# A Fourier, channel-mix and Mish kernel on one core: the ScalarE order of its first stage, the start of its weight conversion, and the first pair of its channel mix

## The chip, the cores and the metric

The kernel runs on one core of a Trainium2 chip. The metric is device time in microseconds (us) for one execution; lower is better. Engines are named as in the profile: PE is TensorE's matmul stream and PEld its weight loads, DVE is VectorE, ACT is ScalarE, POOL is GpSimd, SP is SyncE, whose queue issues nearly all DMAs here. Each engine works through its own queue in order and waits on semaphores of the others.

## The reference

```python
def _attn_ref(x, w_r, w_i, b_r, b_i):                  # x: 4 x 3072 x 256
    X = np.fft.rfft(x, axis=1)
    Yr = Xr @ w_r - Xi @ w_i + b_r
    Yi = Xr @ w_i + Xi @ w_r + b_i
    Yr = np.sign(Yr) * np.maximum(np.abs(Yr) - 0.01, 0.0)
    Yi = np.sign(Yi) * np.maximum(np.abs(Yi) - 0.01, 0.0)
    return np.fft.irfft(Yr + 1j * Yi, n=3072, axis=1)

def _moe_ref(x, mu_k, mu_r, w_k, w_v, w_r):            # channel mix, d_ff 1024
    x_prev = x shifted by one step, zero first
    xk = mu_k * x + (1.0 - mu_k) * x_prev
    xr = mu_r * x + (1.0 - mu_r) * x_prev
    k = np.maximum(xk @ w_k, 0.0)
    return 1.0 / (1.0 + np.exp(-(xr @ w_r))) * (k * k @ w_v)

def _moe2_ref(x, w_in, w_out):                         # Mish, d_ff 2048
    h = x @ w_in
    return (h * np.tanh(log1p(exp(h)))) @ w_out
```

The three run one after the other on 12288 tokens of 256 channels. The weights of the last two are float64 and are turned into float32 on the core.

## The kernel before

Three stages follow each other. **The first stage** does the Fourier part and takes roughly the first 295 us. **The second** (the loop over `t` at line 865) does the channel mix, and **the third** (line 1128) the Mish part. Large products are made from a high part (`h`, rounded to float32r) and a low part (`l`, the rest): three matmuls, high by high, high by low and low by high, stand for one.

The first stage is the loop over `u` at line 667, called a turn here: 48 turns (`NU`), each one group of 256 rows of one batch, and 3 more to finish. The order of a turn is written by hand, and every engine gets its instructions in that order. A turn holds these steps:

- `s2(u + 2)` (line 345): 8 PE matmuls, second half of the DFT, into the single PSUM tile `s2p`. `s2_ev` (365): ACT copies it to `Xf` (line 368), then POOL adds real and imaginary part as a third part of `Xf` (371).
- `high_X(u + 2)` (373): ACT casts `Xf` to its high part `Xh` (375; two buffers). `low_X(u + 1)` (378): DVE subtracts to get `Xl` (381).
- `mix(u)` (392): 18 PE matmuls of `Xh` and `Xl` with the weights `WX`, the first six into `k1p` (one PSUM tile) and the rest into `mxp`. DVE adds the bias to `k1p` (411, result `yt`), and `mix_ev` adds `mxp` (425).
- `above(u)` (427): ACT rectifies `yt` less the threshold into `yc` (429). `shrink(u - 1)` (432): DVE makes `Y` of `yt` and `yc` (435). `swap` (437): three POOL copies exchange halves of `Y` (440 to 442).
- `is1(u - 2)` (444): 2 PE matmuls of the inverse DFT into `i1p`. `is1_ev(u - 3)` (455): ACT copies it to `Cs` (460), and SP stores it.
- In 20 of the turns (`S1_AT`), `s1` (298): 8 PE matmuls of the first half of the DFT of a later group (303). `s1_ev` in the next turn copies them on ACT (311), and SP stores them. Every seventh turn of each batch's twelve (`u % 12 == 6`) has 6 more matmuls in its mix.
- `bg(n)` (85): n steps of a queue of small jobs, 2 and 3 per turn with an `s1`, 1 and 1 in the others. The first jobs load three small tensors. Then `bg_weights` (108) converts nine blocks of the second stage's weights: it loads the first block (`dec_raw`, 512 KB), lets 4 steps pass, and then makes for each block seven DVE instructions (lines 140 to 159), one ACT cast (97) and one DVE subtraction (99).
- From turn 33 on `early(k)` (630) prepares the second stage: inverse DFT of the first tile (`is2`, PE line 509, copied by ACT at 518), its difference `dl` (529), and the two mixed inputs. `shift` (532) makes one of them on DVE (537) and returns a function that makes high part (ACT, line 77) and low part (DVE, line 78) in one step.

After the last mix come three `i1` steps with two `is2` steps between them; this is the drain. Then the second stage begins. It works in pairs `P` of 128-wide columns: `emit_k` (803) makes 12 matmuls per column pair into `kp`, `k_ev` (821) rectifies on ACT (825), squares twice on ACT (835, 836) and subtracts on DVE (837); `emit_v` two pairs later uses the result.

The order of the last steps of a turn, as far as the change touches it:

```python
        if u + 2 < NU:
            s2(u + 2)
        if u > 2:
            is1_ev(u - 3)
        ...
        if u + 2 < NU:
            s2_ev(u + 2)
        ...
        if u < NU:
            mix_ev()
            above(u)
        if u + 2 < NU:
            high_X(u + 2)
```

Of the kernel before, what the change touches and what calls it, by code (L numbers as in the profile page):

```python
# [8 lines left out]
F32 = mybir.dt.float32  # L9
# [3 lines left out]
AF = mybir.ActivationFunctionType  # L13
ALU = mybir.AluOpType
# [15 lines left out]
def kernel(  # L30
# [27 lines left out]
    nc = tc.nc  # L58
# [26 lines left out]
    def bg(n):  # L85

        while n > 0 and bgq:
            try:
                next(bgq[0])
                n -= 1  # L90
            except StopIteration:
                bgq.popleft()
# [15 lines left out]
    def bg_weights(pool, items):  # L108

        if items[0][0].dtype == F32:  # L110
            for src, hi, lo, f in items:
                yield from bg_weight(pool, src, hi, lo, f)
            return
        nxt = raw_load(pool, items[0][0], 2)
        for _ in range(4):
            yield
        for i, (src, hi, lo, f) in enumerate(items):
            raw = nxt
            if i + 1 < len(items):
                nxt = raw_load(pool, items[i + 1][0], 2)  # L120
            yield from bg_weight(pool, src, hi, lo, f, raw=raw)
# [60 lines left out]
    ps1p = ps1.__enter__()  # L182
# [298 lines left out]
    pE = [None]  # L481
# [50 lines left out]
    def shift(t, nm):  # L532
        dl = dl_t[0]
        mu = mk if nm == "xk" else mr
        f = pE[0].tile([128, 2, TA], F32, tag="xf", name="xf", bufs=2)
        for eh in range(2):
            nc.vector.scalar_tensor_tensor(
                out=f[:, eh, :].rearrange("p (m c) -> p m c", m=3), in0=dl[:, eh], scalar=mu[:, eh:eh + 1],
                in1=yv(0)[:, eh], op0=ALU.mult, op1=ALU.add,
            )  # L540
        hl = pE[0].tile([128, 2, 2, TA], F32R, tag=nm, name=nm, bufs=(2 if nm == "xk" else 1))
        (xk_t if nm == "xk" else xr_t)[t] = hl
        return lambda: split(f, hl[:, 0], hl[:, 1])

    warm(3)
    for q in range(8):
# [61 lines left out]
    WK = pkp.tile([128, 2, 2, FK], F32R, tag="WK", name="WK", bufs=1)  # L608
# [16 lines left out]
    def pe_half(t, eh, m0):  # L625
        p = ps1p.tile([128, 2, 256], F32, tag="s1", name="s1p")
        is2(t, eh, p, m0, 2)
        is2_ev(t, eh, m0, 2)

    def early(k):  # L630

        if k == 0:
            load_Dp(0)
            load_D(0)
            load_IF(0)
        elif k == 1:
            pass
        elif k == 2:
            load_D(1)
            load_IF(1)  # L640
        elif k == 3:
            new_yT()
            prefix(0, ps1p.tile([128, 2, 256], F32, tag="s1", name="s1p"))
            later[0] = prefix_ev()
        elif k < 8:
            if k == 4:
                later[0]()
            pe_half(0, (k - 4) // 2, 2 * ((k - 4) % 2))
        elif k == 8:
            delta()  # L650
            load_IF(2)
        elif k == 9:
            later[0] = shift(0, "xk")
        elif k == 10:
            later[0]()
            load_D(2)
        elif k == 11:
            later[0] = shift(0, "xr")
        elif k == 12:
            later[0]()  # L660
        elif k in (14, 15):
            for m0 in (0, 2):
                pe_half(1, k - 14, m0)

    later = {}
    U_E = 32
    for u in range(NU + 3):
        if u + 2 < NU:
            s2(u + 2)
        if u > 2:  # L670
            is1_ev(u - 3)
        if u + 1 < NU:
            low_X(u + 1)
        if 1 <= u <= NU:
            shrink(u - 1)
        while s1_t:
            s1_ev()
        if u + 2 < NU:
            s2_ev(u + 2)
        if 1 <= u <= NU:  # L680
            swap(u - 1)
        if u < NU:
            mix(u)
        if u > 2:
            bg(2 if u in S1_AT else 1)
        if u < NU:
            mix_ev()
            above(u)
        if u + 2 < NU:
            high_X(u + 2)  # L690
        if u + 5 < NU:
            load_A(u + 5)
        if NU <= u < NU + 2:
            early(u - U_E - 2)
        if u == 0:
            load_x(1, 6)
        if u in S1_AT:
            i = 8 + S1_AT[u]
            s1(*divmod(i, 8))
            if i + 3 < 8 * B:  # L700
                load_x(*divmod(i + 3, 8))
        if 2 <= u < NU + 2:
            is1(u - 2)
        if u > 2:
            bg(3 if u in S1_AT else 1)
        if u == U_E:
            p1s.__exit__(None, None, None)
            pEg = tc.tile_pool(name="pE", bufs=1, side="left", reuse_waits="tile")
            pE[0] = pEg.__enter__()
        if U_E < u < NU - 1:  # L710
            early(u - U_E - 1)
# [14 lines left out]
    pap = pa.__enter__()  # L726
    psa = tc.tile_pool(name="psa", bufs=1, space=PSUM, reuse_waits="tile")
    psap = psa.__enter__()
# [6 lines left out]
        src = w_out[q * 256:(q + 1) * 256, :].rearrange("(f p) n -> p f n", p=128)  # L735
        bgq.append(bg_weight(pap, src, WO[:, 2 * q:2 * q + 2, 0, :], WO[:, 2 * q:2 * q + 2, 1, :], 2))

    P3 = ((0, 0), (0, 1), (1, 0))
    g_t = {}

    def emit_h0(P):
# [7 lines left out]
    def h_mm(f0, p):  # L749
# [3 lines left out]
        for dh in range(2):  # L753
            for (w, v) in P3:
                nc.tensor.matmul(  # L755
# [26 lines left out]
    def emit_r(t):  # L782
        hl = xr_t.pop(t)
        p = psap.tile([128, 2, 512], F32, tag="p", name="pp")
        for o in range(2):
            i = 0
            for dh in range(2):
                for (w, v) in P3:
                    nc.tensor.matmul(  # L789
# [12 lines left out]

    def emit_k(P):
        t, i2 = divmod(P, 4)
        hl = xk_t[t]
        p = psap.tile([128, 2, 512], F32, tag="k", name="kp", bufs=2)
        for m in range(2):
            f = 2 * i2 + m
            i = 0
            for dh in range(2):  # L810
                for (w, v) in P3:
                    nc.tensor.matmul(  # L812
                        out=p[:, m, 0:TA], lhsT=WK[:, dh, w, f * 128:(f + 1) * 128], rhs=hl[:, v, dh, :],
                        start=(i == 0), stop=(i == 5),
                    )
                    i += 1
        kp_t[P] = p

    kp_t = {}

    def k_ev(P, then):
        p = kp_t.pop(P)
        v = p[:, :, 0:TA]
        kr = pap.tile([128, 2, TA], F32, tag="kf", name="kr", bufs=2)
        nc.scalar.activation(out=kr, in_=v, func=AF.Relu)
        if then:
            then()
        kh = pap.tile([128, 2, TA], F32R, tag="kh", name="kh", bufs=2)
        kl = pap.tile([128, 2, TA], F32R, tag="kl", name="kl", bufs=2)
        if False:  # L830

            nc.vector.scalar_tensor_tensor(out=kr, in0=v, scalar=0.0, in1=kr, op0=ALU.max, op1=ALU.mult)
            split(kr, kh, kl)
        else:
            nc.scalar.activation(out=kh, in_=kr, func=AF.Square)  # L835
            nc.scalar.activation(out=kr, in_=kr, func=AF.Square)  # L836
            nc.vector.tensor_tensor(out=kl, in0=kr, in1=kh, op=ALU.subtract)  # L837
        kk_t[P] = (kh, kl)

    def emit_v(P):  # L840
# [24 lines left out]
    for t in range(NA + 1):  # L865
# [5 lines left out]
        for i2 in range(4):  # L871
            P = 4 * t + i2
# [6 lines left out]
            then = None  # L879

            if nxt:
# [11 lines left out]
                elif i2 == 2:  # L893
# [5 lines left out]
                    then = shift(t + 1, "xk")  # L899
                else:  # L900
# [4 lines left out]
                    then = shift(t + 1, "xr")  # L905
# [10 lines left out]
            if t == NA - 1 and i2 == 0:  # L916
                hl = x2h_t[0] = w2p.tile([128, 2, 2, 512], F32R, tag="x2h", name="x2h", bufs=1)
# [210 lines left out]
    for P in range(2, 8 * NBLK + LAG):  # L1128
        t, q = divmod(P, 8)
# [111 lines left out]
```

## Time and profile before

| | us |
|---|---|
| median of 3 runs | 1973.39 (1970.25 to 1975.01) |
| the profiled execution's own time | 1974.12 |
| span of the profile, first to last instruction | 1972.3 |
| PE busy | 1946.8 (99%) |
| PEld busy | 1826.0 (93%) |
| DVE busy | 1360.9 (69%) |
| ACT busy | 1065.3 (54%) |
| POOL busy | 137.7 (7%) |

The profile is of one execution. Busy times are sums over the whole span; as matmuls are pipelined and their ends are modelled, a PE shown as busy may still be held up, so the distance from the start of one turn's mix to the start of the next is the better measure. Times in rows count from the span's start. The span is 1.8 us shorter than the execution's own time.

### The profile page before, as it was taken

To read this page: it belongs to the slowest core of one execution; us is meant where nothing else is said; L and a number is where in the kernel's file an instruction comes from. 1 tells how busy PE (TensorE), PEld (TensorE's weight loads), DVE (VectorE), ACT (ScalarE), POOL (GpSimd) and SP (SyncE) were. 2 spreads that over 40 slices of the span, in tenths; PEclk is the share of its full clock that TensorE was granted. 3 is DMA by queue.
4 is the path that set the end of the run, shared out by engine and by line. 5 is a ranking of instruction groups with operands and counts; after the bars stand their busy time and mean duration, and the time that the engine had idled before them with its cause. 6 is when DMAs were issued, how large, how long until landed. Compare 5 with 4: busy or idle time off the path is not lost.

```text
span 1972.3 us, 31894 instructions
## 1 busy us (share of the span) xinstructions
PE 1946.8 (99%) x12658; PEld 1826.0 (93%) x12658; DVE 1360.9 (69%) x2083; ACT 1065.3 (54%) x1598; POOL 137.7 (7%) x236
## 2 busy tenths in 40 slices
PE   7999989999999999999999999999999999999999
PEld 5788879999999999999899999999999999999998
DVE  3688765655656556554587877777877777887785
ACT  3466556666666666666544444444444444444444
POOL 1344440000000000000000000000000000000000
PEclk9999999999999999999999999999999999999999
DMA  9677532221221211210100100010000010000000
GB/s 292 176 235 233 158 100 69 68 62 58 60 62 58 71 60 50 71 58 17 48 23 22 29 26 22 23 33 22 29 27 22 23 33 22 29 27 22 22 12 22
DMA packets 71736, 122.94 MB, mean 62 GB/s; under 512 B 6370, under 2 KB 48580, under 8 KB 71588
## 3 DMA queue, kind: packets, MB, share of 16 engines
q1 hardware_dynamic: 68004, 108.33, 18.7%
q0 software_dynamic: 3584, 12.58, 1.8%
q8 instruction: 100, 1.64, 0.4%
q14 instruction: 48, 0.39, 0.1%
HBM read 70.56 MB, written 50.33 MB: 61 GB/s over the span
## 4 chain that ended last, share of the span: by engine, by line
PE 88%; issue 3%; DVE 3%; ACT 2%; POOL 2%; DMA 2%; SPq 0%; POOLq 0%; ACTq 0%; DVEq 0%
PE h L1057 20%; PE o L1105 18%; PE kp L812 14%; PE vp L850 13%; PE o L1106 9%; PE pp L789 3%; PE p L1057 3%; PE pp L509 3%; ACT Xh L375 1%; DMA XS<-in_x_dram 1%; PE hp L755 1%; PE mxp L408 1%; DVE Xl L381 1%; POOL sw L440 1%; POOL Xf L371 1%
## 5 line engine op out<-in xcount | busy, mean ns | idle before, releaser
L1105 PE MATMUL o<-WO,gh 128*128 128x512 f32 x1536 | 562.0, 394 | 0.0
L1106 PE MATMUL o<-WO,gl 128*128 128x256 f32 x1536 | 430.3, 280 | 0.0
L1057 PE MATMUL h<-xS,WS 128*128 128x256 f32 x2208 | 350.9, 281 | 0.0
L1105 PEld LDWEIGHTS o<-WO,gh 128*128 128x128 f32 x1536 | 288.9, 188 | 43.3
L1070 ACT COPY p1s<-p 128x256 f32<-128x256 f32 x184 | 68.8, 374 | 471.6 <-PE p L1057 470.6
L1057 PEld LDWEIGHTS h<-xS,WS 128*128 128x128 f32 x2208 | 299.6, 188 | 16.1
L812 PE MATMUL kp<-xk,WK 128*128 128x384 f32 x1536 | 294.1, 339 | 0.0
L837 DVE TENSOR_TENSOR kl<-kr,kh 128x768 fp32r<-128x768 f32 x128 | 123.0, 961 | 243.7 <-ACT kr L836 243.7
L1106 PEld LDWEIGHTS o<-WO,gl 128*128 128x128 f32 x1536 | 289.5, 188 | 0.2
L850 PE MATMUL vp<-kh,WV 128*128 128x384 f32 x1024 | 280.3, 335 | 0.0
L812 PEld LDWEIGHTS kp<-xk,WK 128*128 128x128 f32 x1536 | 266.2, 188 | 0.6 <-ACT yT L518 0.2
L1060 DVE TENSOR_TENSOR C<-h,p1s 128x512 f32<-128x512 f32 x184 | 127.2, 692 | 157.9 <-PE h L1057 157.9
L1042 DVE TENSOR_TENSOR gl<-g,gh 128x1024 fp32r<-128x1024 f32 x184 | 223.8, 1216 | 2.1 <-ACT g L1039 2.1
L1038 ACT ACTIVATE gh<-C 128x1024 fp32r<-128x1024 f32 x184 | 195.6, 1063 | 10.8 <-DVE C L1060 10.7
L1039 ACT ACTIVATE g<-C 128x1024 f32<-128x1024 f32 x184 | 193.0, 1049 | 0.0
L1057 PE MATMUL h<-xS,WI 128*128 128x256 f32 x1104 | 189.8, 280 | 0.0
L1060 DVE TENSOR_TENSOR C<-h,wu 128x512 f32<-128x512 f32 x368 | 187.7, 552 | 0.3 <-PE h L1057 0.3
L850 PEld LDWEIGHTS vp<-kh,WV 128*128 128x128 f32 x1024 | 186.7, 188 | 0.0
L850 PE MATMUL vp<-kl,WV 128*128 128x384 f32 x512 | 171.5, 335 | 0.0
L835 ACT ACTIVATE kh<-kr 128x768 fp32r<-128x768 f32 x128 | 108.2, 845 | 100.0 <-PE vp L850 99.9
L1057 PEld LDWEIGHTS h<-xS,WI 128*128 128x128 f32 x1104 | 155.7, 188 | 0.0
L1060 DVE TENSOR_TENSOR wu<-h,C 128x512 f32<-128x512 f32 x184 | 126.6, 688 | 35.3 <-PE h L1057 31.4
(145 smaller groups left out, 2607.9 us busy)
## 6 DMA issues: line engine op xcount, KB each, us to landing
scr<-Cs SPq DMA_DIRECT2D x48, 256.0 KB
D<-scr SPq DMA_DIRECT2D x32, 384.0 KB
x2d<-r POOLq DMA_DIRECT2D x32, 384.0 KB, 2.8
x<-x2d SPq DMA_DIRECT2D x24, 512.0 KB
out_dram<-ob SPq DMA_DIRECT2D x96, 128.0 KB
A<-scr SPq DMA_DIRECT2D x44, 256.0 KB
xs<-in_x_dram SPq DMA_DIRECT2D x24, 384.0 KB
scr<-xs SPq DMA_DIRECT2D x24, 384.0 KB
```

The costliest lines, as they stand in the source:

```text
L812: nc.tensor.matmul(out=p[:, m, 0:TA], lhsT=WK[:, dh, w, f * 128:(f + 1) * 128], rhs=hl[:, v, dh, :], start=(i == 0), stop=(i == 5),)
L835: nc.scalar.activation(out=kh, in_=kr, func=AF.Square)
L837: nc.vector.tensor_tensor(out=kl, in0=kr, in1=kh, op=ALU.subtract)
L850: nc.tensor.matmul(out=p[:, o, 0:TA], lhsT=WV[:, f, w, o * 128:(o + 1) * 128], rhs=v[:, m, :], start=(f == 0 and i == 0), stop=(f == 7 and ...
L1038: nc.scalar.activation(out=gh, in_=c, func=AF.Mish)
L1039: nc.scalar.activation(out=g, in_=c, func=AF.Mish)
L1042: nc.vector.tensor_tensor(out=gl, in0=g, in1=gh, op=ALU.subtract)
L1057: nc.tensor.matmul(out=out, lhsT=a(l), rhs=xS[:, v, b, :], start=(n == 0), stop=(n == 2))
L1060: nc.vector.tensor_tensor(out=out, in0=x0, in1=x1, op=ALU.add)
L1070: nc.scalar.copy(out=p1s, in_=p1)
L1105: nc.tensor.matmul(out=o[m], lhsT=gh[:, m2, ms], rhs=WO[:, f], start=(f == 0), stop=False)
L1106: nc.tensor.matmul(out=o[m][:, 0, :], lhsT=gl[:, m2, ms], rhs=WO[:, f, 0, :], start=False, stop=(f == 15))
```

## The change

Five things move; one load of PE work moves from the second stage to the first.

1. `high_X(u + 2)`, ACT's cast, stands ahead of `mix_ev` and `above(u)` instead of behind them.
2. `is1_ev(u - 3)`, ACT's copy to `Cs` and the store behind it, stands behind `s2_ev(u + 2)` instead of in front of `s1_ev`.
3. The weight conversion lets 10 steps of its queue pass after its first load instead of 4.
4. In `early`, high and low part of the second stage's first inputs are separate steps, the low part one turn behind the high part.
5. The 12 matmuls of the first pair of `kp` and their rectification are issued at `u == 48`, ahead of the last two `i1` steps, into PSUM tiles of the first stage.

The core of the diff:

```diff
         nxt = raw_load(pool, items[0][0], 2)
-        for _ in range(4):
+        for _ in range(10):
             yield
...
         (xk_t if nm == "xk" else xr_t)[t] = hl
-        return lambda: split(f, hl[:, 0], hl[:, 1])
+        def high():
+            nc.scalar.copy(out=hl[:, 0], in_=f)
+        def low():
+            nc.vector.tensor_tensor(out=hl[:, 1], in0=f, in1=hl[:, 0], op=ALU.subtract)
+        return high, low
...
         elif k == 9:
-            later[0] = shift(0, "xk")
+            later[0], later[1] = shift(0, "xk")
         elif k == 10:
             later[0]()
             load_D(2)
         elif k == 11:
-            later[0] = shift(0, "xr")
+            later[1]()
+            later[0], later[1] = shift(0, "xr")
         elif k == 12:
             later[0]()
+        elif k == 13:
+            later[1]()
...
+    def first_k():
+        ps = [ps1p.tile([128, 512], F32, tag=g, name="k0p", bufs=n)[:, 0:TA] for g, n in (("s2", 1), ("mx", 2))]
+        k_mm(0, ps)
+        kr = pE[0].tile([128, 2, TA], F32, tag="xf", name="kr0", bufs=2)
+        for m, p in enumerate(ps):
+            nc.scalar.activation(out=kr[:, m, :], in_=p, func=AF.Relu)
+        kr_0.append(kr)
...
     for u in range(NU + 3):
         if u + 2 < NU:
             s2(u + 2)
-        if u > 2:
-            is1_ev(u - 3)
...
             s2_ev(u + 2)
+        if u > 2:
+            is1_ev(u - 3)
...
+        if u + 2 < NU:
+            high_X(u + 2)
         if u < NU:
             mix_ev()
             above(u)
-        if u + 2 < NU:
-            high_X(u + 2)
...
             early(u - U_E - 2)
+        if u == NU:
+            first_k()
```

`k_mm` holds the matmul loop that `emit_k` had; `emit_k` and `k_ev` skip for pair 0 what `first_k` has done. For all other pairs they issue the same instructions as before.

**ACT, from the rectification of turn 7 to the copy of turn 9's `s2`.** The number in a name is that of its buffer; `yc_770` is turn 7's rectified tile before, `yc_769` after. Before:

```order
L429 ACTIVATE yc_770<-yt_748 128x512
L375 CAST Xh_772<-Xf_739 128x768
L460 COPY Cs_788<-i1p_776 128x512
L368 COPY Xf_795<-s2p_783 128x2x256
L429 ACTIVATE yc_827<-yt_804 128x512
L375 CAST Xh_829<-Xf_795 128x768
L460 COPY Cs_852<-i1p_841 128x512
L311 COPY xs_524<-s1p_833 96x512
L311 COPY xs_524<-s1p_836 96x512
L368 COPY Xf_862<-s2p_847 128x2x256
```

After:

```order
L429 ACTIVATE yc_769<-yt_745 128x512
L368 COPY Xf_785<-s2p_776 128x2x256
L460 COPY Cs_788<-i1p_773 128x512
L375 CAST Xh_817<-Xf_785 128x768
L429 ACTIVATE yc_820<-yt_797 128x512
L97 CAST WK_321<-dec_v_658 128x512
L311 COPY xs_524<-s1p_824 96x512
L311 COPY xs_524<-s1p_827 96x512
L368 COPY Xf_849<-s2p_837 128x2x256
L460 COPY Cs_852<-i1p_832 128x512
L375 CAST Xh_887<-Xf_849 128x768
```

The cast of `Xf` now follows its own copy with only `Cs` between, ahead of the rectification `yc` instead of behind it; `Cs` is behind the copy to `Xf`. The weight cast (L97) is in another turn.

**DVE, turns 4 and 5, where the weight conversion begins.** L140 is the first instruction on a loaded block. Before:

```order
L381 TENSOR_TENSOR Xl_538<-Xf_479,Xh_514 128x768
L435 SCALAR_TENSOR_TENSOR Y_540<-yt_488,yc_512 128x512
L411 TENSOR_TENSOR yt_554<-k1p_553,BIAS_97 128x512
L140 TENSOR_SCALAR dec_v_576<-dec_raw_528 128x512
L425 TENSOR_TENSOR yt_554<-mxp_552,yt_554 128x512
L144 SCALAR_TENSOR_TENSOR dec_v_576<-dec_raw_528,dec_v_576 128x512
```

After:

```order
L381 TENSOR_TENSOR Xl_535<-Xf_476,Xh_511 128x768
L435 SCALAR_TENSOR_TENSOR Y_537<-yt_488,yc_514 128x512
L411 TENSOR_TENSOR yt_554<-k1p_553,BIAS_97 128x512
L425 TENSOR_TENSOR yt_554<-mxp_552,yt_554 128x512
L381 TENSOR_TENSOR Xl_596<-Xf_542,Xh_574 128x768
L435 SCALAR_TENSOR_TENSOR Y_602<-yt_554,yc_577 128x512
L411 TENSOR_TENSOR yt_619<-k1p_618,BIAS_97 128x512
L425 TENSOR_TENSOR yt_619<-mxp_617,yt_619 128x512
L140 TENSOR_SCALAR dec_v_658<-dec_raw_528 128x512
L144 SCALAR_TENSOR_TENSOR dec_v_658<-dec_raw_528,dec_v_658 128x512
```

L140 moved past five instructions, from the middle of turn 4 to the end of turn 5.

**PE, from the last turn's `i1` to the first matmuls of the second stage.** Before:

```order
L450 MATMUL i1p_3107<-Y_3040,WF_95 128x512
L509 MATMUL s1p_3118<-ift_2485,D_2483 128x96 x2
L509 MATMUL s1p_3124<-ift_2485,D_2483 128x96 x2
L450 MATMUL i1p_3130<-Y_3076,WF_95 128x512
L509 MATMUL s1p_3135<-ift_2485,D_2483 128x96 x2
L509 MATMUL s1p_3139<-ift_2485,D_2483 128x96 x2
L450 MATMUL i1p_3143<-Y_3112,WF_95 128x512
L812 MATMUL kp_3161<-xk_2879,WK_321 128x384 x12
L812 MATMUL kp_3186<-xk_2879,WK_321 128x384 x12
```

After:

```order
L450 MATMUL i1p_3107<-Y_3036,WF_95 128x512
L509 MATMUL s1p_3118<-ift_2485,D_2483 128x96 x2
L509 MATMUL s1p_3124<-ift_2485,D_2483 128x96 x2
L686 MATMUL k0p_3130<-xk_2879,WK_321 128x384 x6
L686 MATMUL k0p_3131<-xk_2879,WK_321 128x384 x6
L450 MATMUL i1p_3147<-Y_3073,WF_95 128x512
L509 MATMUL s1p_3152<-ift_2485,D_2483 128x96 x2
L509 MATMUL s1p_3156<-ift_2485,D_2483 128x96 x2
L450 MATMUL i1p_3160<-Y_3109,WF_95 128x512
L686 MATMUL kp_3188<-xk_2879,WK_321 128x384 x12
```

Twelve matmuls of the first pair (`k0p`) moved ahead of the last two `i1` steps; the number of matmuls is the same.

## Rows read from the trace of the kernel before

**Rows 1.** Stretches: us, PE, PEld, DVE, ACT, POOL busy (count), PEclk, DMA share, GB/s
```profile
75.00:82.00 7.00, 6.49 (x17) 4.37 (x18) 4.54 (x7) 3.79 (x8) 2.28 (x4) 0.51 0.61 177
...
125.00:150.00 25.00, 24.92 (x161) 20.73 (x160) 20.68 (x33) 14.74 (x30) 11.72 (x20) 1.00 0.78 238
```

**Rows 2.** Timeline, turns 7 and 8, PE (start, us, engine, line, operation)
```profile
86.69 0.48 PE L408 MATMUL k1p<-WX,Xh 128*128 128x256 f32 x2
...
88.92 1.02 PE L450 MATMUL i1p<-Y,WF 128*128 128x512 f32 x2
89.78 1.05 PE L352 MATMUL s2p<-MC,A 128*128 128x128 f32 x8
...
90.59 0.48 PE L408 MATMUL k1p<-WX,Xh 128*128 128x256 f32 x2
```

**Rows 3.** Timeline, turns 10 to 12: in brackets, idle before and what ended it
```profile
102.12 0.48 PE L408 MATMUL k1p<-WX,Xh 128*128 128x256 f32 x2
...
105.47 0.97 PEld L352 LDWEIGHTS s2p<-MC,A 128*128 128x128 f32 x8 [0.92 <-ACT Xf L368]
...
106.39 0.48 PE L408 MATMUL k1p<-WX,Xh 128*128 128x256 f32 x2
...
112.02 0.48 PE L408 MATMUL k1p<-WX,Xh 128*128 128x256 f32 x2
```

**Rows 4.** Timeline, turn 34, ACT and DVE
```profile
225.07 0.63 ACT L429 ACTIVATE yc<-yt 128x512 f32<-128x512 f32 x1 [2.11 <-DVE yt L425]
225.61 0.82 ACT L375 CAST Xh<-Xf 128x768 fp32r<-128x768 f32 x1
226.46 0.96 DVE L381 TENSOR_TENSOR Xl<-Xf,Xh 128x768 fp32r<-128x768 f32 x1 [1.48 <-ACT Xh L375]
227.34 0.69 DVE L435 SCALAR_TENSOR_TENSOR Y<-yt,yc 128x512 f32<-128x512 f32 x1
228.73 0.69 DVE L425 TENSOR_TENSOR yt<-mxp,yt 128x512 f32<-128x512 f32 x1
229.51 0.63 ACT L429 ACTIVATE yc<-yt 128x512 f32<-128x512 f32 x1 [2.12 <-DVE yt L425]
```

**Rows 5.** Timeline, turns 4 to 6, where the first weight block comes in
```profile
64.54 0.43 SPq L105 DMA_DIRECT2D dec_raw<-in_moe_w_k_dram  x1
69.98 0.48 PE L408 MATMUL k1p<-WX,Xh 128*128 128x256 f32 x2
70.67 0.43 DVE L140 TENSOR_SCALAR dec_v<-dec_raw 128x512 int32<-128x512 int32 x1 [4.18 <-DMA dec_raw<-in_moe_w_k_dram]
75.51 3.73 PE L303 MATMUL s1p<-xs,FC 96*96 96x256 f32 x8 [3.15 <-ACT xs L311]
82.06 0.48 PE L408 MATMUL k1p<-WX,Xh 128*128 128x256 f32 x2
```

**Rows 6.** Timeline, turns 2 and 3, weight loads of PE
```profile
52.69 0.30 PEld L408 LDWEIGHTS k1p<-WX,Xh 128*128 128x128 f32 x2 [1.15 <-DVE yt L411]
...
60.87 1.54 PEld L303 LDWEIGHTS s1p<-xs,FC 96*96 96x96 f32 x8 [0.34 <-ACT xs L311]
```

**Rows 7.** Timeline, turn 41 to the last turn
```profile
255.40 0.48 PE L408 MATMUL k1p<-WX,Xh 128*128 128x256 f32 x2
...
262.82 1.58 DVE L435 SCALAR_TENSOR_TENSOR Y<-yt,yc 128x512 f32<-128x512 f32 x1
263.12 0.72 POOL L371 TENSOR_TENSOR Xf<-Xf 128x256 f32<-128x256 f32 x1
272.45 0.96 DVE L78 TENSOR_TENSOR xk<-xf,xk 128x768 fp32r<-128x768 f32 x1 [2.22 <-ACT xk L77]
286.63 0.76 PE L408 MATMUL k1p<-WX,Xh 128*128 128x256 f32 x2 [2.77 <-DVE yt L411]
```

**Rows 8.** Chain of waits, drain and start of the second stage (start, us, what)
```profile
291.37 0.87 PE s1p L509 x8
...
295.37 4.20 PE kp L812 x24
```

More of the change, by code (lines that the diff above doesn't have):

```diff
@@ L663, in early, with k_mm @@
                 pe_half(1, k - 14, m0)
+    P3 = ((0, 0), (0, 1), (1, 0))
+    kp_t, kr_0 = {}, []
+    def k_mm(P, ps):
+        t, i2 = divmod(P, 4)
+        hl = xk_t[t]
+        for m, p in enumerate(ps):
+            f = 2 * i2 + m
+            i = 0
+            for dh in range(2):
+                for (w, v) in P3:
+                    nc.tensor.matmul(
+                        out=p, lhsT=WK[:, dh, w, f * 128:(f + 1) * 128], rhs=hl[:, v, dh, :],
+                        start=(i == 0), stop=(i == 5),
+                    )
+                    i += 1
+    def first_k():
+        ps = [ps1p.tile([128, 512], F32, tag=g, name="k0p", bufs=n)[:, 0:TA] for g, n in (("s2", 1), ("mx", 2))]
+        k_mm(0, ps)
+        kr = pE[0].tile([128, 2, TA], F32, tag="xf", name="kr0", bufs=2)
+        for m, p in enumerate(ps):
+            nc.scalar.activation(out=kr[:, m, :], in_=p, func=AF.Relu)
+        kr_0.append(kr)
     later = {}
@@ L736 @@
         bgq.append(bg_weight(pap, src, WO[:, 2 * q:2 * q + 2, 0, :], WO[:, 2 * q:2 * q + 2, 1, :], 2))
-    P3 = ((0, 0), (0, 1), (1, 0))
     g_t = {}
@@ L804, in emit_k @@
         t, i2 = divmod(P, 4)
[L805 to L819, printed above, removed]
-    def k_ev(P, then):
[L822 to L827, printed above, removed]
+        if P:
+            p = kp_t[P] = psap.tile([128, 2, 512], F32, tag="k", name="kp", bufs=2)
+            k_mm(P, [p[:, m, 0:TA] for m in range(2)])
+    def k_ev(P, then):
+        if P:
+            kr = pap.tile([128, 2, TA], F32, tag="kf", name="kr", bufs=2)
+            nc.scalar.activation(out=kr, in_=kp_t.pop(P)[:, :, 0:TA], func=AF.Relu)
+        else:
+            kr = kr_0[0]
+        for step in then or ():
+            step()
         kh = pap.tile([128, 2, TA], F32R, tag="kh", name="kh", bufs=2)
         kl = pap.tile([128, 2, TA], F32R, tag="kl", name="kl", bufs=2)
[L830 to L837, printed above, removed]
+        nc.scalar.activation(out=kh, in_=kr, func=AF.Square)
+        nc.scalar.activation(out=kr, in_=kr, func=AF.Square)
+        nc.vector.tensor_tensor(out=kl, in0=kr, in1=kh, op=ALU.subtract)
         kk_t[P] = (kh, kl)
```

## The prediction

> **What bounds the kernel now.** The page's totals say PE 99% busy, which hides what this change is about, since all of it lies in the first 300 of 1972 us. I therefore read the first stage turn by turn: in the timeline, the first `k1p` matmul of each turn marks where it starts, and two marks give its length. The reader should compare that length with what the same matmuls take when nothing holds them. Turn 7 is such a turn [rows 2]: mix 88.92 - 86.69 = 2.23 us, `i1` 89.78 - 88.92 = 0.86, `s2` 90.59 - 89.78 = 0.81, together 3.90. With an `s1` it is 112.02 - 106.39 = 5.63 [rows 3]. Every turn that is longer has a wait in it, and the timeline names who ended it.
>
> Four places are longer.
>
> Turn 5 lasts 82.06 - 69.98 = 12.08 us instead of 5.63 [rows 5]. DVE reached L140, the first instruction on the first weight block, 4.18 us before the block had landed; it landed at 70.65, 6.1 us after its issue. DVE's queue stood still meanwhile, ACT waited for DVE, PE's `s1` waited 3.15 us for ACT's copies, and its 8 matmuls then took 3.73 us. In that stretch the granted clock was 0.51 [rows 1], the 1.2 GHz level, after PE had stood idle for those 3.15 us.
>
> Turn 10, and every other steady turn without an `s1`, lasts 106.39 - 102.12 = 4.27 instead of 3.90: PE's load for `s2` waits for ACT's copy to `Xf`, because `s2p` is a single tile [rows 3].
>
> From turn 33 a turn is 229.51 - 225.07 = 4.44 us, though it holds no more matmuls than turn 7. That is a ring through two engines [rows 4]: `yc` to the cast `Xh` 0.54, to DVE's `Xl` 0.85, to `Y` 0.88, over the first bias sum to the second sum 1.39, to the next `yc` 0.78. The sum is 4.44, the turn's length. The ring exists because the cast stands behind `yc` in ACT's queue, although it needs nothing of it; and `Xl` stands ahead of `Y` in DVE's.
>
> The end of the stage, from turn 41 at 255.40 to the end of the first two pairs at 295.37 + 4.20 = 299.57, takes 44.17 us [rows 7, 8]. DVE stands still there 2.22 us before the low part of `xk`, since the high part is issued just ahead of it on ACT, and PE waits 2.77 us for DVE before the last mix.
>
> **The change, part by part.**
>
> *Cast ahead of `yc`, `Cs` behind `Xf`.* No instruction is added. The cast now waits for its `Xf` and for the end of `mix(u)`, which still reads the older of the two `Xh` buffers; the end of the mix comes before the sum that `yc` waits for, so the cast starts earlier by that sum and `yc`, and it is off the ring. What is left of the ring is 4.44 - 0.54 - 0.85 = 3.05 us if DVE does `Xl` while ACT makes `yc`, below 3.90 [rows 4]. So PE sets the pace at 3.90: turns 33 to 35 give 3 x 0.54 = 1.6 us. In the steady part ACT reaches the copy to `Xf` earlier by the `yc` wait and by `Cs`; the wait of 0.92 is 0.37 beyond the turn's own length, and six turns (10, 13, 16, 22, 25, 28) give 6 x 0.37 = 2.2 us [rows 3]. In turns 2 and 3 the same lateness of DVE and ACT shows as waits of 1.15 and 0.34 us [rows 6], together 1.5 us. What is moved back by this: `yc` gets at most one cast of 0.82 later, behind it `Y` and the swap; `i1` reads `Y` only two turns later, so that is covered by a turn of at least 3.90. `Cs` gets later, and behind it on SP's queue its store and the next load of `A`; `A` is used three turns later, 11.7 us or more, against 6.1 us that the 512 KB weight block took [rows 5]. I cost both at nothing.
>
> *Conversion later.* L140 stands five DVE instructions further back, at the end of turn 5. It was wanted at 70.65 - 4.18 = 66.47; a turn later is 66.47 + 5.63 = 72.1, against the landing at 70.65 with the load in the same place. The margin is 1.4 us and the second sum of turn 5 on top. So DVE no longer stands, PE does not idle and the clock does not drop: turn 5 goes from 12.08 to 5.63, which is 6.45 us. Cost: the conversion ends some three turns later, around turn 34; that adds the last block's few DVE instructions to turns where DVE has room. The bounds are 0 (the block comes later still) and 6.45; I take 6.45.
>
> *Low parts a turn later.* DVE no longer waits 2.22 us for ACT's cast. The low part of `xk` now shares turn 44 with the two mixing instructions of `xr`.
>
> *First pair ahead of the drain.* The same 12 matmuls, half of 4.20 = 2.10 us [rows 8], stand between `is2` and `i1`, where PE otherwise waits for the last `yc`, `Y` and swap. Nothing waits for the last `Cs` at once.
>
> Together the last two and the cast act on the end of the stage. Its PE work: turns 41, 43, 44 at 3.90; turn 42 with 6 more matmuls of 2.23 / 18, 4.64; turns 45 and 46 without `s2`, 3.09 each; then mix 2.23, three `i1` 2.58, `is2` 2 x 0.87 and the two pairs 4.20 [rows 2, 8]. That is 33.3 us against 44.17, so at most 10.9 us. The lower bound is what the sight of a 2.22 and a 2.77 us wait gives, 5.0 [rows 7]. DVE is close to PE there: its sums, `Xl` and `Y` are 0.69 + 0.69 + 0.96 + 0.69 = 3.0 us a turn, and turn 44 has two more pieces, so I take 9.5.
>
> Sum: 6.45 + 1.6 + 2.2 + 1.5 + 9.5 = 21.3 us. Against the profiled execution's 1974.1 that is 1952.8, against the median of 1973.4 it is 1952.1. I say **1952 us**. The two later stages issue the same work and keep their time.
>
> **The rivals.**
>
> *DVE becomes the bound.* DVE is busy 20.68 of 25 us [rows 1], so in three steady turns (4.27 + 2 x 5.63 = 15.53) 12.8 us; PE alone needs 15.16. When it collides with POOL this can go: at 262.82 `Y` took 1.58 us instead of 0.69 while POOL added `Xf` [rows 4, 7]. If the new order makes `Y` meet POOL in every turn, three turns cost DVE 3 x 0.89 more, 15.5 us: the steady 2.2 us are lost, and seven turns at the end lose 7 x 0.89 = 6.2. Gain 12.9, time 1960.5. Against it: in 125 to 150 us both engines are that busy and it is POOL that is stretched. The Trainium skill has this as a rule (page "SBUF — State Buffer", section "Who interferes with whom"): a VectorE instruction with two SBUF inputs and a GpSimd instruction that reads SBUF keep each other out for their whole length. The 1.58 us row agrees with that rule. Chance 0.13.
>
> *The first weight block is still late.* The load moves with the turn, or lands later than 6.1 us because turns 2 and 3 are shorter and transfers are closer together. Then turn 5 keeps its wait: 1952 + 6.45 = 1958.5. For it speaks the margin of 1.4 us. Chance 0.08.
>
> *The cast is early in the order only.* If it waits for the older buffer or for POOL as long as it did for `yc`, the ring stays, and only the conversion, the 1.5 us of turns 2 and 3 and half of the end are won: 6.45 + 1.5 + 4.7 = 12.7, time 1961. Against it: the mix that it waits for ends before the sum that `yc` waits for. Chance 0.05.
>
> *Slower: a ring through SP.* `Cs` is now last on ACT, its store follows on SP's queue, and the load of `A` stands behind that store; `A` feeds the `s2` of three turns later, which feeds `Xf` and `Cs` again. In three turns, 15.16 us, `s2` takes 0.81 and four steps of ACT and SP under 0.85 each, so a load of `A` may take 10.9 us from issue to landing before it decides anything. The stage has seven such periods between turns 9 and 30. To eat the gain it must take 10.9 + 21.3 / 7 = 13.9 us; at 15 us it costs 7 x 4.1 = 28.7, time 1981. The trace shows 6.1 us for a block twice as large, with DMA engines 78% busy [rows 1, 5]. Chance 0.02.
>
> **How the numbers follow.** The forecast has 0.72. Its own range is 1946 (everything to PE's bound, 22.7 us, some small waits of 0.04 to 0.4 us that I left out, and 2 us spread of the runs) to 1957 (the end of the stage at its lower bound). To hold 8 in 10 it reaches over the rivals at 1958.5 and 1960.5: 1946 to 1962. A measurement of this kernel tells 0.3% from no change, that is below 1967.5 for faster; all but the last rival and mishaps lie there: faster 0.94, same 0.04, slower 0.02.
>
> **What would show it.** Right: turn 5 at about 5.6 us, no wait of L140 on `dec_raw`, no stretch at the lower clock around 75 us; steady turns without `s1` and turns 33 to 35 at 3.9; `Xh` ending before `yc` begins; from turn 41 to the end of the second pair about 34 to 35 us; the second stage's later turns unchanged. Wrong: turns still at 4.27 or 4.44 (then see what DVE's `Y` takes, and what PE's weight loads wait for), L140 waiting in turn 5, or loads of `A` landing after `s2` wants them.

## The result, and the profile after

| | before | after |
|---|---|---|
| median of 4 runs each, us | 1972.77 (1970.25 to 1975.01) | 1951.76 (1950.31 to 1955.14) |
| profiled execution, us | 1974.1 | 1950.83 |
| its span, us | 1972.3 | 1949.1 |

The ratio is 0.9896, with a 95% interval of 0.9878 to 0.9915: about 1% faster. The forecast was 1952.0.

The first thing to read is again the distance from one turn's first `k1p` to the next. On the timeline of the kernel after, turns 5, 10 and 34 to 35 (columns: start, us, engine, line, operation, and in brackets the idle time before and who ended it):

```profile
67.57 0.48 PE L408 MATMUL k1p<-WX,Xh 128*128 128x256 f32 x2
...
69.80 1.89 PE L303 MATMUL s1p<-xs,FC 96*96 96x256 f32 x8
...
70.61 0.42 DVE L140 TENSOR_SCALAR dec_v<-dec_raw 128x512 int32<-128x512 int32 x1
...
73.19 0.48 PE L408 MATMUL k1p<-WX,Xh 128*128 128x256 f32 x2
...
92.98 0.48 PE L408 MATMUL k1p<-WX,Xh 128*128 128x256 f32 x2
...
96.88 0.48 PE L408 MATMUL k1p<-WX,Xh 128*128 128x256 f32 x2
...
212.22 0.48 PE L408 MATMUL k1p<-WX,Xh 128*128 128x256 f32 x2
...
214.58 0.83 ACT L375 CAST Xh<-Xf 128x768 fp32r<-128x768 f32 x1 [1.00 <-PE mxp L408]
214.65 0.69 DVE L425 TENSOR_TENSOR yt<-mxp,yt 128x512 f32<-128x512 f32 x1
...
215.37 0.63 ACT L429 ACTIVATE yc<-yt 128x512 f32<-128x512 f32 x1
215.45 1.04 DVE L381 TENSOR_TENSOR Xl<-Xf,Xh 128x768 fp32r<-128x768 f32 x1
...
216.12 0.48 PE L408 MATMUL k1p<-WX,Xh 128*128 128x256 f32 x2
```

Turn 5 is 73.19 - 67.57 = 5.62 us, where before it was 12.08 [rows 5]; L140 has no wait in brackets, and the 8 `s1` matmuls take 1.89 us instead of 3.73. Turn 10 is 96.88 - 92.98 = 3.90 against 4.27 [rows 3], turn 34 is 3.90 against 4.44 [rows 4]. The cast now begins at the end of the mix, together with DVE's second sum, and `Xl` follows it while ACT makes `yc`: the step of 0.54 from `yc` to cast is out of the ring.

The same is seen without any marks in the groups of instructions of 100 to 175 us (count, then busy us and mean ns, then the idle time of the engine just before and its releaser). Before:

```profile
L381 DVE TENSOR_TENSOR Xl<-Xf,Xh 128x768 fp32r<-128x768 f32 x14 | 13.4, 957 | 13.1 <-ACT Xh L375 13.1
```

and after:

```profile
L381 DVE TENSOR_TENSOR Xl<-Xf,Xh 128x768 fp32r<-128x768 f32 x15 | 14.2, 949 | 0.0
```

DVE stood 13.1 of these 75 us waiting for the cast, and no longer does. In the stretch of turn 5 (PE, PEld, DVE, ACT, POOL busy, PEclk, DMA share, GB/s) after, PE does not pause and the granted clock stays at the 2.4 GHz level, where before it fell to 0.51 [rows 1]:

```profile
67.60:73.20 5.60, 5.60 (x39) 4.72 (x38) 3.83 (x7) 3.57 (x7) 1.93 (x4) 1.00 1.04 288
```

At the end of the stage one hold is left. The timeline of turns 44 and 45 after:

```profile
257.22 1.16 DVE L548 TENSOR_TENSOR xk<-xf,xk 128x768 fp32r<-128x768 f32 x1
...
258.30 1.27 DVE L537 SCALAR_TENSOR_TENSOR xf<-dl,small,yT 128x384 f32<-128x384 f32 x2
...
259.03 1.14 POOL L371 TENSOR_TENSOR Xf<-Xf 128x256 f32<-128x256 f32 x1 [0.40 <-ACT Xf L368]
...
259.50 1.49 DVE L381 TENSOR_TENSOR Xl<-Xf,Xh 128x768 fp32r<-128x768 f32 x1
...
262.33 0.47 PE L408 MATMUL k1p<-WX,Xh 128*128 128x256 f32 x2 [0.99 <-DVE yt L411]
```

The last row is the start of turn 46: PE has stood 0.99 us for DVE. `Xl` takes 1.49 us here and not its usual 0.95, beside POOL's sum, which runs until 260.17. Then the chain of waits behind it (start, us, what), with the first pair's 12 matmuls inside the drain:

```profile
268.59 0.87 PE s1p L509 x8
269.45 2.12 PE k0p L686 x12
271.57 0.86 PE i1p L450 x2
272.43 0.86 PE s1p L509 x8
273.30 0.89 PE i1p L450 x2
274.18 2.08 PE kp L686 x12
276.26 2.08 PE pp L825 x12
```

Nothing of PE's chain is idle from 268.59 on. The second pair ends at 276.26, so the stretch from turn 41 (241.76) is 34.50 us, against 44.17 [rows 7, 8].

Where the 23.2 us of span went, by those marks:

| stretch | before | after | gained | forecast |
|---|---|---|---|---|
| turn 0 | 4.84 | 4.00 | 0.84 | none |
| turns 1 to 4 | 21.53 | 19.94 | 1.59 | 1.5 |
| turn 5 | 12.08 | 5.62 | 6.46 | 6.45 |
| turns 6 to 32 | 137.74 | 135.12 | 2.62 | 2.2 |
| turns 33 to 40 | 35.60 | 33.45 | 2.15 | 1.6 |
| turn 41 to end of second pair | 44.17 | 34.50 | 9.67 | 9.5 |

The sum is 23.3. What follows the second pair takes 1672.7 us before and 1672.8 after, so the rest of the kernel kept its time. The places and sizes stand. Which part of the change pays for each of them is another question, and that is what the experiments ask.

### The profile page after: what moved, and what is told of

The parts are those of the page before. It is cut to its first block, busy times and chain, and to the rows that moved or that the text cites. A ratio compares the mean times of both kernels' runs of the same rounds, so it can differ in the third digit from the quotient of the medians.

```text
span 1949.1 us, 31847 instructions
## 1 busy us (share of the span) xinstructions
PE 1934.9 (99%) x12658; PEld 1821.8 (93%) x12658; DVE 1359.1 (70%) x2083; ACT 1072.4 (55%) x1599; POOL 131.7 (7%) x236
## 4 chain that ended last, share of the span: by engine, by line
PE 98%; DMA 1%; DVE 0%; ACT 0%; SPq 0%; issue 0%; DVEq 0%
PE h L1078 20%; PE o L1126 18%; PE kp L686 14%; PE vp L871 14%; PE o L1127 9%; PE mxp L408 4%; PE pp L825 3%; PE p L1078 3%; PE pp L509 3%; PE s1p L303 3%; PE s2p L352 2%; PE i1p L450 2%; PE k1p L408 2%; PE hp L791 1%; DMA yc<-in_w_i_dram 0%; PE h0p L791 0%
```

## The experiments

In a diff, "after" or "before" says which kernel it starts from. Gains are told against the median of before in the same series (1972.47, 1972.31, 1974.68 and 1973.45 us in the four series), lengths of turns from each kernel's profile.

**Conversion later, alone** (before).

```diff
-        for _ in range(4):
+        for _ in range(10):
```

> The kernel before with one edit: the weight conversion lets 10 steps pass instead of 4. Theory (turn 5 was long because DVE stood at L140 for the first weight block, and PE then ran at the lower clock): turn 5 falls from 12.1 us to 5.7 to 6.0 us, no wait of L140 on dec_raw, no stretch at half clock around 75 us, all other turns as before (4.27 without s1, 4.44 in turns 33 to 35); time about 6.2 us less than before, 1966 to 1967. Rival (the block lands later still, or another DMA takes its place as the wait): turn 5 stays over 8 us and the gain is under 4 us.

Measured: 1969.91, ratio 0.9983 [0.9973, 0.9993], a gain of 2.6 us. Timeline:

```profile
67.48 0.48 PE L408 MATMUL k1p<-WX,Xh 128*128 128x256 f32 x2
...
70.52 0.61 DVE L140 TENSOR_SCALAR dec_v<-dec_raw 128x512 int32<-128x512 int32 x1
...
73.11 0.48 PE L408 MATMUL k1p<-WX,Xh 128*128 128x256 f32 x2
...
102.43 0.48 PE L408 MATMUL k1p<-WX,Xh 128*128 128x256 f32 x2
...
103.96 0.69 DVE L99 TENSOR_TENSOR WK<-dec_v,WK 128x512 fp32r<-128x512 f32 x1 [2.00 <-ACT WK L97]
...
108.42 0.48 PE L408 MATMUL k1p<-WX,Xh 128*128 128x256 f32 x2
```

Turn 5 is 5.63 without a wait of L140, as expected. But the other turns are not as before: turn 12 is 5.99 instead of 5.67, as the conversion's DVE steps now fall into other turns of the old order, and one of them waits 2.00 us for ACT. Turns 12 to 14 take 16.01 us instead of 15.56, and turns 6 to 40 take 176.38 instead of 173.34: 3.0 of the 6.45 us are paid back there. The expected gain of 6.2 was missed; the rival's gain of under 4 us came, but not for its reason, a long turn 5.

**Conversion back** (after): the same line, 10 to 4.

> The changed kernel with 4 steps again, all else changed. Theory: L140 stands in turn 4 again and waits some 4 us; yc and the copies to xs stand behind it on ACT, so turn 5 is long again (9 to 12 us) with a stretch at half clock; 3.5 to 6.5 us more than the change, 1955 to 1958. Rival (the new ACT order alone covers the wait, as the cast no longer stands behind yc): turn 5 under 6.5 us, time within 1 us of the change.

Measured: 1954.25, ratio 0.9911 [0.9894, 0.9929]. In the profile, turn 5 is 77.53 - 68.11 = 9.42 and every other turn but turn 0 is as after. Timeline:

```profile
61.21 0.54 SPq L105 DMA_DIRECT2D dec_raw<-in_moe_w_k_dram  x1
...
67.52 0.43 DVE L140 TENSOR_SCALAR dec_v<-dec_raw 128x512 int32<-128x512 int32 x1 [3.36 <-DMA dec_raw<-in_moe_w_k_dram]
...
72.37 2.96 PE L303 MATMUL s1p<-xs,FC 96*96 96x256 f32 x8 [1.88 <-ACT xs L311]
```

So with the rest in place the later conversion is worth 3.8 us in the profile and 2.5 by the medians (3.5 to 6.5 were expected), not 6.45.

**Cast ahead of `yc`, alone** (before).

```diff
             bg(2 if u in S1_AT else 1)
+        if u + 2 < NU:
+            high_X(u + 2)
         if u < NU:
             mix_ev()
             above(u)
-        if u + 2 < NU:
-            high_X(u + 2)
```

> The kernel before with one edit: the cast ahead of yc. Theory (the cast off the ring is the main edit, the others are worth little once it is made): turns 33 to 35 at 3.9 us and turns without s1 at 3.9 to 4.0 us; turn 5 about 9.4 us as with 4 steps in the changed kernel; the end longer than 34.4 us by the low parts and the first pair, 2 to 4 us; time 1956 to 1961. Rival (the five edits need each other): over 1964, with turns of 4.2 us and more left.

Measured: 1957.96, ratio 0.9929 [0.9909, 0.9949], a gain of 14.4 us. All steady turns are at PE's length, and the end of the stage is 39.7 us, 5.2 more than after where 2 to 4 were expected. Even turn 5, in which the conversion stands where it stood, is down to 6.97; 9.4 was expected. Timeline and stretch:

```profile
61.27 0.43 SPq L105 DMA_DIRECT2D dec_raw<-in_moe_w_k_dram  x1
...
66.99 0.43 DVE L140 TENSOR_SCALAR dec_v<-dec_raw 128x512 int32<-128x512 int32 x1 [2.59 <-DMA dec_raw<-in_moe_w_k_dram]
...
71.83 1.97 PE L303 MATMUL s1p<-xs,FC 96*96 96x256 f32 x8 [1.10 <-ACT xs L311]
```

```profile
68.00:75.00 7.00, 5.89 (x39) 4.82 (x38) 6.58 (x12) 4.58 (x12) 2.05 (x3) 1.00 0.80 235
```

Three kernels make a series: L140 waits 4.18, 3.36 and 2.59 us (before, conversion back, cast alone), PE then stands 3.15, 1.88 and 1.10 us before its `s1`, which takes 3.73, 2.96 and 1.97. After these waits the granted clock is 0.51 [rows 1], 0.76 (over 71 to 78 us) and 1.00. So in the last kernel turn 5 is 1.34 us beyond 5.63, little more than its wait; in the other two the half clock is added.

**Cast back** (after): the cast behind `mix_ev` and `above` again, the edit above in reverse.

> The changed kernel with the cast behind yc again; Cs stays behind Xf, the other parts stay. Theory (ring yc, Xh, Xl, Y, sums): turns 33 to 35 are 4.4 us again, turn 1 over 4 us, from turn 41 to the end of the second pair 3 to 6 us more than 34.4; steady turns without s1 between 3.9 and 4.1, as Cs no longer stands before Xf; time 6 to 10 us more than the change. Rival (moving Cs did the work): turns 33 to 35 stay at 3.9 and the time within 2 us.

Measured: 1971.65, ratio 0.9996 [0.9986, 1.0005]: nearly the whole gain is lost, twice what was expected. The end of the stage is 40.09 us, 5.6 more than after, as expected; but steady turns without an `s1` take 4.50, not 3.9 to 4.1, and turns 33 to 40 take mostly 4.97, longer than the 4.44 of before. Timeline:

```profile
216.25 0.63 ACT L429 ACTIVATE yc<-yt 128x512 f32<-128x512 f32 x1 [2.64 <-DVE yt L425]
...
216.79 0.82 ACT L375 CAST Xh<-Xf 128x768 fp32r<-128x768 f32 x1
...
217.64 0.96 DVE L381 TENSOR_TENSOR Xl<-Xf,Xh 128x768 fp32r<-128x768 f32 x1 [1.48 <-ACT Xh L375]
...
218.17 1.02 POOL L371 TENSOR_TENSOR Xf<-Xf 128x256 f32<-128x256 f32 x1 [1.96 <-ACT Xf L368]
218.52 1.22 DVE L435 SCALAR_TENSOR_TENSOR Y<-yt,yc 128x512 f32<-128x512 f32 x1
```

The ring is back (`yc`, cast, `Xl`, `Y`), and `Y` takes 1.22 instead of 0.69 because POOL's sum of `Xf` runs beside it; 4.44 + 0.53 = 4.97. POOL takes 1.02 itself instead of 0.72: its sum begins 0.43 us before `Xl` ends, and `Y` ends 0.55 us after the sum does. The Trainium skill ("SBUF — State Buffer", "Who interferes with whom") says that a VectorE instruction with two inputs in SBUF and a GpSimd instruction that reads SBUF contend for a shared port pair; these rows agree with it.

**`Cs` back ahead** (after), and **cast and `Cs` both back** (after).

```diff
+        if u > 2:
+            is1_ev(u - 3)
         if u + 1 < NU:
             low_X(u + 1)
...
-        if u > 2:
-            is1_ev(u - 3)
         if 1 <= u <= NU:
             swap(u - 1)
```

> The changed kernel with the copy to Cs ahead of the copies of s1 again. Theory (the cast off the ring is what matters, ACT has room for one copy of 0.58 us): turns without s1 stay at 3.9 to 4.0 us, turns 33 to 35 at 3.9, time within 1.5 us of the change. Rival (Cs ahead of Xf made PE's s2 wait): turns without s1 at 4.2 to 4.3 us, six of them, 2 us more.

> The changed kernel with both ACT moves undone: cast behind yc, Cs ahead of the copies of s1; later conversion, low parts and first pair stay. Theory (Cs behind Xf makes the ring longer as long as the cast is on it): turns 33 to 35 at 4.4 to 4.7 us as in the kernel before, less than with the cast alone undone (4.4 to 5.4), time 3 to 6 us below that run. Rival (Cs has no part in it): the same turns and time as with the cast alone undone.

Measured, one run each: 1950.31 and 1964.51. Both theories hold in their turns: turns 33 to 35 are at 3.90 and at 4.44 to 4.68. With the kernel after and the one with only the cast back this makes a table of four, all with the other parts in place:

| | `Cs` behind `Xf` | `Cs` ahead, as before |
|---|---|---|
| cast ahead of `yc` | 1951.76 | 1950.31 |
| cast behind `yc` | 1971.65 | 1964.51 |

Moving `Cs` is worth nothing beside the new cast, and costs some 7 us beside the old one, because `Xf` and so POOL's sum come earlier and meet `Y`. In the groups of 100 to 175 us, of cast back and then of both back:

```profile
L371 POOL TENSOR_TENSOR Xf<-Xf 128x256 f32<-128x256 f32 x14 | 14.8, 1056 | 34.5 <-ACT Xf L368 34.5
...
L435 DVE SCALAR_TENSOR_TENSOR Y<-yt,yc 128x512 f32<-128x512 f32 x14 | 11.7, 836 | 0.0
```

```profile
L371 POOL TENSOR_TENSOR Xf<-Xf 128x256 f32<-128x256 f32 x14 | 12.0, 859 | 38.7 <-ACT Xf L368 38.7
...
L435 DVE SCALAR_TENSOR_TENSOR Y<-yt,yc 128x512 f32<-128x512 f32 x14 | 9.6, 685 | 0.0
```

The cast is worth 1964.51 - 1950.31 = 14.2 us with `Cs` in its old place, as in the run of the cast alone.

**Low parts right behind the high parts** (after).

```diff
             later[0]()
+            later[1]()
             load_D(2)
         elif k == 11:
-            later[1]()
...
-        elif k == 13:
             later[1]()
```

> The changed kernel with the low parts right behind the high parts again. Theory: DVE stands for about 1 us or less, as the cast comes earlier now, or it moves work out of turns 44 and 46; the end is within 1.5 us of 34.4 us. Rival (the low parts' wait of 2.2 us, twice, is what made the end long): 3 us or more longer.

Measured, one run: 1952.74; the end of the stage takes 37.96 us, 3.46 more than after, so the rival holds in its size; DVE stands 1.42 us ahead of each low part, not 2.2. Turns 44 and 46 are 4.83 and 5.25 us instead of 3.90 and 2.87. In turn 46 DVE stands for the cast of `xr`, and PE then for DVE before turn 47:

```profile
264.05 0.96 DVE L548 TENSOR_TENSOR xr<-xf,xr 128x768 fp32r<-128x768 f32 x1 [1.42 <-ACT xr L545]
...
267.23 0.48 PE L408 MATMUL k1p<-WX,Xh 128*128 128x256 f32 x2 [2.00 <-DVE yt L411]
```

**First pair behind the drain again** (after without `first_k`; pair 0 as every other).

```diff
-        if u == NU:
-            first_k()
...
-        if P:
+        if True:
```

> The changed kernel without the first pair ahead of the drain. Theory: PE waits for the last yc, Y and swap by 0.4 to 1 us before the last i1; the end is longer by that. Rival (the drain held PE for all of the pair's 2.1 us): 1.8 us or more longer.

Measured, one run: 1952.92; the end takes 278.34 - 243.09 = 35.25, which is 0.75 more. The chain of waits shows where:

```profile
271.85 1.25 PE s1p L509 x8
273.10 1.07 PE i1p L450 x2
274.17 4.17 PE kp L686 x24
```

Without the 12 matmuls between them, `s1` and `i1` of the drain take 1.25 and 1.07 us instead of 0.87 and 0.86: PE is held a few tenths at a step, no more.

**Entry of `xr` a turn later** (after): its mixing in turn 45, high part in 46, low part in turn 48, so that turn 44 has one piece fewer.

```diff
             later[1]()
-            later[0], later[1] = shift(0, "xr")
         elif k == 12:
-            later[0]()
+            later[0], later[1] = shift(0, "xr")
         elif k == 13:
-            later[1]()
+            later[0]()
         elif k in (14, 15):
+            if k == 14:
+                later[1]()
```

> The changed kernel with the mixed input xr made one turn later each (mixing in turn 45, high part in 46, low part in 48), so that DVE does not hold both in turn 44. Theory (turn 45 is 1.2 us longer than its matmuls because DVE is late): turn 45 at 3.1 to 3.3 us, turns 46 and 47 longer by at most 0.5 together, the end 0.5 to 1.2 us shorter; too little to tell from the change in time. Rival (the delay only moves to turn 46 or into the drain): the end as long as in the change or longer.

Measured: 1951.34, ratio 0.9901 [0.9886, 0.9916], no different from after. Turn 45 falls to 3.25, turn 46 rises to 3.93, and the end takes 34.43 against 34.50: the hold is only moved, as the rival has it.

**The two low parts of turns 44 and 46 on POOL** (after).

```diff
-            nc.vector.tensor_tensor(out=hl[:, 1], in0=f, in1=hl[:, 0], op=ALU.subtract)
+            (nc.vector if t else nc.gpsimd).tensor_tensor(out=hl[:, 1], in0=f, in1=hl[:, 0], op=ALU.subtract)
```

> The changed kernel with the two low parts of turns 44 and 46 made on POOL instead of DVE. Theory (in turns 44 and 45 DVE has too much, 1.2 us of PE time): turn 45 at 3.1 to 3.4 us, turns 46 and 47 at most 0.5 us longer, the stretch from turn 41 to the end of the second pair 33.3 to 33.9 us instead of 34.4; about 0.7 us in all, too little to tell by time. Rival (POOL's subtraction, three times as long as its sum of 0.7 us, keeps DVE's Xl and Y out or makes the last swap late): the stretch as long as in the change or longer.

Measured: 1953.86, ratio 0.9897 [0.988, 0.9913], no faster than after. Turn 45 is 5.28 instead of 4.25 and turn 46 is 4.16 instead of 2.87, so the end takes 37.09, 2.6 us longer than after: the rival holds. Timeline:

```profile
257.52 3.93 DVE L537 SCALAR_TENSOR_TENSOR xf<-dl,small,yT 128x384 f32<-128x384 f32 x2
...
258.51 1.84 POOL L548 TENSOR_TENSOR xk<-xf,xk 128x768 fp32r<-128x768 f32 x1
...
260.32 0.72 POOL L371 TENSOR_TENSOR Xf<-Xf 128x256 f32<-128x256 f32 x1
```

DVE's two mixing instructions took 1.27 us after (258.30 in the rows of turn 44) and 3.93 here, beside the subtraction that POOL took over in 1.84 and POOL's own next sum. DVE got its work back as a wait.

**One more sum on DVE in turns 6 to 39**, first input in PSUM, then both in SBUF (after). Nothing uses the added sum.

```diff
+        mixes.append(0)
+        if 6 < len(mixes) <= 40:
+            j = p1p.tile([128, 2, D], F32, tag="junk", name="junk", bufs=1)
+            nc.vector.tensor_tensor(out=j, in0=p, in1=BIAS[:, 1], op=ALU.add)
```

In the second kernel `in0=BIAS[:, 0]`.

> The changed kernel with one more DVE sum per turn in turns 6 to 39, 128x512, one input in PSUM, one in SBUF; its result is used by nothing. Theory (PE sets the pace, DVE has some 15% left): DVE rises to nearly all of the time, and the stretch of turns 9 to 30 grows by 0 to 4 us. Rival (DVE is at its bound already): 0.69 us in each of 22 turns, 15 us.

> The same with both inputs in SBUF. If an added sum costs the same whichever memory its inputs are in, the stretch of turns 9 to 30 is as long as in the run with one input in PSUM, to 1 us. If two SBUF inputs and POOL keep each other out, it is 3 us or more longer than that run, and POOL's or DVE's instructions in it are stretched.

Measured, one run each: 1957.69 and 1960.36. Turns 9 to 30 take 119.28 and 120.16 us, against 113.17 after: 6.1 and 7.0 more, between the two expectations. Three turns take 16.2 instead of 15.16, with 3 x 0.68 = 2.0 us added, so DVE has about 1.0 us to spare in three turns. In 100 to 175 us of the first kernel:

```profile
100.00:175.00 75.00, 72.40 (x475) 61.62 (x474) 70.27 (x108) 46.39 (x85) 34.73 (x56) 1.00 0.75 227
```

DVE is busy 70.27 of 75 us (63.10 after), and PE 72.40 (75.00 after). The 0.9 us between the two kernels is too little to say what the second input costs.

## Why the prediction was right, and where it was not

**The sum and the place.** 21.3 us were forecast for 23.2 in the span and 21.0 in the medians. Every stage's term came out within 0.6 us but for turn 0, which the forecast did not have: kernels with the same instructions there differ by more than its 0.84 us (last section), so that part of the gain is luck. Turn 1 is not steady either: it took 3.04 to 4.92 us in kernels with the cast ahead of `yc`, so the 1.15 us that the forecast read from its wait cannot be confirmed by one profile. What "some small waits of 0.04 to 0.4 us that I left out" and turns 36 to 40, which the sum left out, give is the rest.

**The ring.** "The cast starts earlier by that sum and `yc`, and it is off the ring" holds: `Xh` begins 0.79 us ahead of `yc` at 214.58, DVE's idle time ahead of `Xl` goes from 13.1 to 0.0, and turns 33 to 35 are at 3.90. Turns 36 to 40, which hold 4 more PE matmuls of the second stage's inputs, are at 4.35 without a wait of PE.

**Turn 5, a wrong owner.** "So DVE no longer stands, PE does not idle and the clock does not drop: turn 5 goes from 12.08 to 5.63, which is 6.45 us" is right in its outcome and wrong in giving all of it to the later conversion. The cast alone takes turn 5 to 6.97, so either of the two parts would remove up to 5.1 of the 6.45. The step that failed is "with the load in the same place": SP issued the block's load 69.98 - 64.54 = 5.44 us ahead of turn 5 before, and 68.34 - 61.27 = 7.07 us ahead of it with the cast alone, since the store of `Cs` ahead of it in SP's queue, which waits for ACT, went out at 57.09 instead of 60.37. These 1.63 us match the 1.59 by which L140's wait fell. The later conversion is worth 1.3 (6.97 to 5.62) to 3.8 us (conversion back) beside the cast, and 2.6 by the medians without it.

**Steady turns, half wrong.** I gave the gained 0.37 a turn to the earlier `yc` wait "and by `Cs`". `Cs` has no share: put back, it changes no turn from turn 2 on by more than 0.2 us. Without the cast it is a loss (the table of four), and I costed at nothing what it does to POOL: it lets POOL's sum start earlier, beside `Y`.

**The end.** 9.5 forecast, 9.67 measured. Its owners: cast 44.17 - 39.7 = 4.5; low parts 3.46; first pair 0.75; together 8.7. The other 1.0 fits the clock, which the forecast did not price here. Before, PE stood 2.77 us ahead of the last mix [rows 7] and then ran at the 1.2 GHz level:

```profile
286.63:290.63 4.00, 4.00 (x19) 3.91 (x20) 2.03 (x4) 1.10 (x2) 1.82 (x5) 0.58 0.19 66
```

In the kernel with the conversion alone PE stood 2.79 us there, the clock stayed at 1.00, and from that mix to the end of the second pair it took 11.80 us instead of 12.94. So some 1.1 us of the 9.67 hang on a fall that the same wait brought in one execution and not in the other. I had looked for the first pair to fill the drain; without it PE is held there for only 0.4 and 0.2 us. The 1.2 us between the 33.3 of PE's work and 34.50 is mostly turn 45. "Turn 44 has two more pieces" does cost about what the forecast kept for it, but 0.54 of the 0.99 us that PE waits there is `Xl` beside POOL's sum.

**The rivals.** DVE as the bound did not come in the steady turns, but its mechanism is real: it lengthens `Xl` in turn 44 after, `Y` beside POOL took 1.22 in the kernel with the cast back, and the spare time of DVE is 1.0 us in three turns. The weight block was not late: with its load at 60.67, and a landing 6.3 us after issue as in the kernel with the conversion back (61.21 to 67.52), it is there some 3.6 us ahead of L140 at 70.61; the margin was 1.4 in the forecast. The cast was not early in the order only: it waits 1.0 us for the mix and not for `yc`. A ring through SP was not seen: between 43 and 280 us neither PE nor its loads wait for `A`; the only wait for a DMA is one of 0.2 us, for another tensor.

**The parts and their sum.** The parts' single worths don't add up (2.6 and 14.4 alone; 2.5 and 19.9 undone, by the medians). Lengths of stretches from each kernel's profile show where, from turn 2 to the end of the second pair:

| | turns 2 to 4 | turn 5 | turns 6 to 32 | turns 33 to 40 | end | sum |
|---|---|---|---|---|---|---|
| before | 17.28 | 12.08 | 137.74 | 35.60 | 44.17 | 246.87 |
| conversion alone | 17.28 | 5.63 | 140.34 | 36.04 | 42.49 | 241.78 |
| cast alone | 16.89 | 6.97 | 135.12 | 33.45 | 39.74 | 232.17 |
| after | 16.89 | 5.62 | 135.12 | 33.45 | 34.50 | 225.58 |
| conversion back | 16.89 | 9.42 | 135.13 | 33.45 | 34.50 | 229.39 |
| cast back | 16.89 | 5.63 | 142.61 | 39.09 | 40.09 | 244.31 |
| cast and `Cs` back | 17.27 | 5.63 | 140.32 | 36.02 | 39.07 | 238.31 |

The cast alone makes turns 6 to 40 what they are after. With the old order of ACT the later conversion costs 3.0 us in them, with the new one nothing; and without the cast, `Cs` behind `Xf` costs 5.4 there. These two make the cast's undoing dearer than its gain alone. Why the conversion's steps cost more at their new place in the old order was not followed further than the wait of 2.00 us.

## To carry to other kernels

In an in-order queue, look for an instruction that needs nothing of the one ahead of it but stands behind that one's wait: here one cast, moved up past one activation, carried about 14 of 21 us with no work removed. Forecast each stage from the length that the bound engine needs, and don't split the gain among the parts of a change by the wait that each is aimed at: two parts may remove the same wait, and one part may hurt without the other. A copy that is made earlier also starts whatever follows it earlier; ask what that will run beside.

## What was not expected of the hardware

The first turn's length varies between kernels whose instructions are the same up to there: 4.00 us after, 3.94 with the first pair behind the drain, 4.69 with the entry of `xr` a turn later, 3.05 with the low parts on POOL, all of which differ only at the end of the stage. The granted clock of 25 to 50 us was 0.86 before and 0.93 after. From 43.7 to 44.5 us it was 0.50 after, and with the low parts back:

```profile
43.70:44.50 0.80, 0.80 (x9) 0.80 (x9) 0.80 (x2) 0.28 (x1) 0.45 (x1) 1.00 1.03 379
```

In the profiles of all kernels turn 0 took 3.04 to 4.84 us and ended at 45.8 to 49.8 us: 3.04 or 3.05 where its first `k1p` pair took 0.48 us (2.4 GHz), 3.64 to 4.84 where it took 0.77 or 0.78 (1.2 GHz). That is up to 4 us of the span, and the four runs of the kernel after differ by 4.8, so a difference of less than that in a single run says nothing; the lengths of the steady turns do, which agree to some 0.02 us. Whether the first turn is what makes the runs of one kernel differ is not shown, as each kernel has one profile.

The second is how far a meeting of POOL and DVE reaches: 0.53 us more for `Y` lengthened most of turns 33 to 40 by as much each, and two mixing instructions went from 1.27 to 3.93 us beside a subtraction and a sum on POOL.
